# A channel-attention kernel: other piece sizes in its first pass, and other first stores and reads

## The chip, the cores and the metric

The kernel runs on one core of a Trainium2 chip. The metric is device time in microseconds, from one execution's start to its end. The kernel before takes 733.99 us as the median of three runs (733.06, 733.99, 737.35).

## The reference

The input x has 384 x 384 pixels of 384 channels in bf16. Each channel gets one factor from its mean and its maximum over all pixels, and x is multiplied by these factors. No pixel can be scaled before all have been seen.

```python
def reference(x, w1, w2):            # x (1, 384, 384, 384), w1 (384, 96), w2 (96, 384)
    B, H, W, C = x.shape
    xf = x.reshape(B, H * W, C)
    gap = jnp.mean(xf, 1)
    gmp = jnp.amax(xf, 1)
    h_a = gap @ w1
    h_a = h_a * (h_a > 0)
    h_m = gmp @ w1
    h_m = h_m * (h_m > 0)
    scale = _sigmoid(h_a @ w2 + h_m @ w2)
    return x * scale[:, None, None, :]
```

## The kernel before

**Tiling.** The pixels lie on 128 partitions, and each partition has 1,152 of them. One pixel on all partitions is called a row here: 128 x 384 values, 98,304 bytes. x is 1,152 rows, 113.25 MB. On-chip memory does not hold that, so there are two passes.

**First pass** (lines 366 to 399). One list, `loads`, is made from the constants at the top and then walked in order. SyncE issues each load (line 369). TensorE adds its rows up with matmuls against a column of ones (line 274, groups of four rows, three matmuls each). VectorE takes the maximum of its rows with an accumulator `acc` in the tensor `hole`, 11 rows wide, in instructions of 6 and 5 rows by turns (line 311, `larger`). Toward the end the accumulator is folded to 6 and then 3 rows (`FOLDS`: key, how many loads are left; value, the new width), and then to one.

**Slots.** Three slots of 44 rows hold what is loaded; the trace calls them x_88, x_89 and x_90, and they are used in turn. `FILLS` has one entry per use of a slot: a first tuple of packed pieces (16 rows, a pair of two packed groups of 8) and a second of plain pieces. The plain pieces of the fills, 804 rows, are read again in the second pass (`AGAIN`), and so are the 11 rows that the accumulator starts from; everything else stays on the chip. A piece may be loaded once all engines that read what was in its rows are done, and the order of SyncE's queue is that of the list: a load that waits holds up the ones behind it. Besides, at most eight DMAs are under way: a load also waits for the landing of the eighth before it.

**Packing** (`pack`, line 316). 144 rows stay on the chip in a shorter code. For a pair of groups ScalarE takes the bytes apart (line 321), TensorE joins the high parts (line 334, three groups of six matmuls into one bank, each taken out by ScalarE at line 344), ScalarE copies the low bytes (line 339; with the second of these copies the slot's 16 rows are read for the last time) and tests the result (lines 341 and 346). The working space for that lies in the first rows of `room`, which take plain rows later (`ROOM_PIECES`), after the last pair.

**What stays.** 44 rows in each slot (`STAYING`), 35 in `room`, 10 beside the accumulator (`LATE_PIECES`, put into the list at the place that `LATE_AT` names: slot, and how many of its pieces go before), 16 in PSUM. The list ends with the third slot's pieces. The last three loads are summed in another form (`tail_sums`).

**Between the passes.** After the last maximum: a fold to one row, transposes, two small products and a sigmoid (lines 404 to 425) give `scale_bc`.

**Second pass** (lines 481 to 532). VectorE multiplies a piece in place (line 430), ScalarE's queue issues its store (line 446), and SyncE reads the next block into the slot once the store has landed (line 454). `FIRST_STORES` cuts the first slots and the room into stores, `FIRST_READS` the first reload, taken from the slot's end. Later ones are of 44 rows. The packed rows are unpacked between them.

Scheduling of the first pass is left to the framework, within each engine by the order of the program; for the second pass it is written out by hand.

Of the kernel before, what the change touches and what calls it, by code (L numbers as in the profile page):

```python
# [54 lines left out]

PSUM_PIECES = (4, 12)
FILLS = (
    ((16,), ()), ((), (44,)), ((), (44,)), ((16,), ()), ((), (44,)), ((), (44,)),
    ((16,), ()), ((), (44,)), ((), (44,)), ((16,), ()), ((), (44,)), ((), (44,)),
    ((16,), ()), ((), (44,)), ((), (44,)), ((16,), ()), ((), (43,)), ((), (40,)),  # L60
    ((), (36,)), ((), (36,)), ((16,), (27,)), ((), (28,)), ((), (28,)), ((16,), (26,)),
    ((), (24,)), ((), (23, 21)), ((16,), (16,)), ((), (16,)),
)
ROOM_PIECES = (10, 9, 5, 6, 5)
STAYING = ((17, 15, 12), (11, 11, 11, 11), (6, 4, 3, 4, 3, 6, 3, 3, 3, 6, 3))
ROOM_LOADS = 2
LATE_AT = (2, 1)
LATE_PIECES = (5, 5)

FOLDS = {7: 6, 1: 3}  # L70

AGAIN = (44,) * 18 + (12,)
FIRST_STORES = ((1, 2, 3, 4, 4, 6, 8, 8, 8), (8, 8, 9, 9, 10), (10, 11, 14))
FIRST_READS = ((8, 8, 8, 10, 10), (44,))
LEAD = 2
ROOM_TURN = 2
ACC_STORES_AT = 3
# [8 lines left out]
def kernel(  # L86
# [158 lines left out]
    def pieces_of(block, pieces, buf):  # L245
        j = 0
        for m in pieces:
            loads.append((block, j, j + m, buf, j, ()))
            j += m
        assert j == block[1]  # L250

    for s, pieces in enumerate(STAYING):
        if s == ROOM_LOADS:
            pieces_of(room_b, ROOM_PIECES, room)
        n = len(loads)
        pieces_of(stay_b[s], pieces, slots[s])
        if s == LATE_AT[0]:
            j = 0
            for i, m in enumerate(LATE_PIECES):
                loads.insert(n + LATE_AT[1] + i, (late_b, j, j + m, late, j, ()))  # L260
                j += m
# [95 lines left out]
    def fold(n, to):  # L357
        while n > to:
            h = min(n // 2, n - to)
            larger(acc[:, 0:h, :], acc[:, 0:h, :], acc[:, n - h:n, :])  # L360
            n -= h
        return n
# [3 lines left out]
    for i, (block, lo, hi, buf, at, groups) in enumerate(loads):  # L366
# [14 lines left out]
        if i == len(PSUM_PIECES):  # L381
# [5 lines left out]
            continue  # L387
        if n_loads - i in FOLDS:
            width = fold(width, FOLDS[n_loads - i])
            parts, turn = PARTS[width], 0  # L390
# [91 lines left out]
    order.insert(ROOM_TURN, (room_b, None))  # L482
    stores, reads = list(FIRST_STORES), list(FIRST_READS)
    n_turns = len(order) + len(again)
# [92 lines left out]
```

## Time and profile before

The profiled execution took 734.48 us, with a span of 732.6 us and 1.9 us around it.

| what | number |
| --- | --- |
| median of three runs | 733.99 us (733.06 to 737.35) |
| profiled execution, its span | 734.48 us, 732.6 us |
| bytes moved | 193.51 MB read, 113.25 MB written; 419 GB/s over the span |
| VectorE busy | 556.5 us (76%) |
| ScalarE busy | 250.8 us (34%) |
| TensorE busy | 162.8 us (22%) |
| chain of waits, by kind | DMA 58%, VectorE 34%, issue 2% |
| the last load of the first pass lands | 274.03 us |
| `scale_bc` is ready | 280.34 us |
| first store is issued | 280.75 us |

How to read it: times within the execution count from the span's start. "Busy" is time in which an engine works on an instruction. The chain of waits is followed from the last instruction back to what released it, step by step, and so names what the end of the execution hung on. A load's landing is the last of sixteen completion signals, one from each DMA engine.

### The profile page before, as it was taken

What the parts mean: (1) busy time and instruction counts of PE and PEld (TensorE: products, weight loads), DVE (VectorE), ACT (ScalarE), POOL (GpSimd) and SP (SyncE); (2) the same over time, 40 slices, a digit from 0 to 9 for tenths busy, and PEclk for the clock granted to TensorE, in tenths of its full rate; (3) what the DMA queues carried; (4) which work ended last, traced back from release to release, by engine and by line L of the source; (5) the groups of instructions that cost most, each with busy time, mean ns of one, the idle gap of its engine ahead of it and who ended that gap; (6) DMA issues with size and microseconds to landing.
All of it is one profiled execution on the core that took longest, in us unless ns stands there. A gap on an engine that the chain in (4) does not pass through costs nothing.

```text
span 732.6 us, 3124 instructions
## 1 busy us (share of the span) xinstructions
PE 162.8 (22%) x1069; PEld 52.0 (7%) x1078; DVE 556.5 (76%) x422; ACT 250.8 (34%) x135; POOL 0.7 (0%) x6
## 2 busy tenths in 40 slices
PE   3664656554756561000000000000000000000000
PEld 0221212111211120000000000000000000000000
DVE  6689989899999998979276777277667666667930
ACT  4998889853997400002011011011110011111100
POOL 0000000000000000000000000000000000000000
PEclk9968878677675755555555555555555555555555
DMA  9999999999999988999999999999999999999997
GB/s 378 440 431 414 431 415 412 400 426 427 427 424 422 417 329 306 386 442 425 437 439 424 435 436 441 421 437 440 424 437 437 423 437 439 423 437 427 434 438 339
DMA packets 19391, 306.95 MB, mean 419 GB/s; under 512 B 2512, under 2 KB 3120, under 8 KB 8368
## 3 DMA queue, kind: packets, MB, share of 16 engines
q1 hardware_dynamic: 12896, 193.52, 62.5%
q10 hardware_dynamic: 6480, 113.25, 36.2%
q8 instruction: 8, 0.13, 0.1%
q14 instruction: 7, 0.06, 0.0%
HBM read 193.51 MB, written 113.25 MB: 419 GB/s over the span
## 4 chain that ended last, share of the span: by engine, by line
DMA 58%; DVE 34%; issue 2%; ACT 0%; SPq 0%; PE 0%; DVEq 0%; ACTq 0%
DMA x<-in_x_dram 37%; DMA out_dram<-x 21%; DVE hole L311 20%; DVE x L430 12%; DVE room L430 1%; DVE hole L430 1%; ACT room L464 0%; SPq L369 0%; DVE room L470 0%; DVEq L535 0%; PE bank_a L424 0%; ACT scale_bc L425 0%; DVE small L419 0%; PE bank_a L418 0%; PE bank_a L422 0%
## 5 line engine op out<-in xcount | busy, mean ns | idle before, releaser
L430 DVE TENSOR_TENSOR x<-x,scale_bc 128x16896 bf16<-128x16896 bf16 (+9 forms) x34 | 191.5, 5660 | 94.6 <-DMA x<-in_x_dram 93.5
L311 DVE TENSOR_TENSOR hole<-hole,x 128x1920 bf16<-128x1920 bf16 (+2 forms) x211 | 235.7, 1191 | 20.0 <-DMA x<-in_x_dram 18.6
L464 ACT ACTIVATE room<-room 128x3072 uint16<-128x3072 uint8 x18 | 49.7, 2763 | 360.2 <-DVE x L430 309.4
L274 PE MATMUL bank_a<-x,small 128*1 128x512 bf16 (+1 forms) x816 | 92.7, 481 | 49.4 <-DMA x<-in_x_dram 48.6
L334 PE MATMUL bank_b<-room 128*128 128x512 bf16 x153 | 59.9, 526 | 51.9 <-ACT room L324 22.4
L321 ACT CAST room<-x 128x3072 bf16<-128x3072 uint8 x18 | 48.7, 2750 | 45.1 <-DMA x<-in_x_dram 45.1
L339 ACT COPY room<-x 128x3072 uint8<-128x3072 uint8 x18 | 49.3, 2737 | 0.0
L470 DVE TENSOR_TENSOR room<-room,hole 128x3072 uint16<-128x3072 uint16 x18 | 31.6, 1758 | 23.0 <-ACT room L464 23.0
L341 ACT ACTIVATE room<-room,w_sb 128x6144 uint8<-128x6144 bf16 x9 | 48.7, 5407 | 0.0
L430 DVE TENSOR_TENSOR room<-room,scale_bc 128x3072 bf16<-128x3072 bf16 (+3 forms) x21 | 38.9, 1861 | 0.6
L274 PEld LDWEIGHTS <-small 128*1 128x1 bf16 x861 | 29.1, 95 | 131.8 <-issue 116.0
L467 DVE TENSOR_SCALAR hole<-room 128x768 uint16<-128x768 uint16 x90 | 25.7, 353 | 0.0
L346 ACT ACTIVATE room<-room,w_sb 128x3072 bf16<-128x3072 uint16 x9 | 25.7, 2853 | 0.0
L334 PEld LDWEIGHTS <-room 128*128 128x128 bf16 x162 | 19.0, 119 | 90.9 <-issue 85.7
L344 ACT ACTIVATE room<-bank_b 128x512 uint16<-128x512 f32 x27 | 15.9, 590 | 1.7 <-PE bank_b L334 1.7
L324 ACT ACTIVATE room<-x 128x1536 bf16<-128x1536 bf16 x9 | 13.3, 1478 | 0.0
L470 DVE TENSOR_TENSOR hole<-hole 128x768 uint16<-128x768 uint16 x18 | 10.0, 558 | 0.6
L299 ACT COPY w_sb<-bank_a 65x128 f32<-65x128 f32 x2 | 0.5, 262 | 25.3 <-PE bank_a L274 24.8
L311 DVE TENSOR_TENSOR hole<-hole,room 128x1920 bf16<-128x1920 bf16 (+2 forms) x7 | 7.6, 1152 | 0.0
L379 DVE COPY kept_ps<-x 128x768 uint32<-128x768 uint32 (+1 forms) x2 | 3.5, 1760 | 4.2 <-DMA x<-in_x_dram 4.2
L274 PE MATMUL bank_a<-room,small 128*1 128x512 bf16 (+1 forms) x27 | 4.1, 543 | 4.2 <-DMA room<-in_x_dram 4.2
L311 DVE TENSOR_TENSOR hole<-hole 128x1920 bf16<-128x1920 bf16 (+2 forms) x6 | 4.9, 823 | 0.1
(46 smaller groups left out, 29.8 us busy)
## 6 DMA issues: line engine op xcount, KB each, us to landing
x<-in_x_dram SPq DMA_DIRECT2D x27, 4224.0 KB, 24.4
out_dram<-x ACTq DMA_DIRECT2D x19, 4224.0 KB, 24.0
x<-in_x_dram SPq DMA_DIRECT2D x11, 1536.0 KB, 12.2
x<-in_x_dram SPq DMA_DIRECT2D x2, 3456.0 KB, 16.7
out_dram<-room ACTq DMA_DIRECT2D x2, 3072.0 KB, 31.4
x<-in_x_dram SPq DMA_DIRECT2D x2, 2688.0 KB, 16.7
x<-in_x_dram SPq DMA_DIRECT2D x4, 1056.0 KB, 11.4
out_dram<-room ACTq DMA_DIRECT2D x1, 4224.0 KB, 29.5
```

The source lines that it names most:

```text
L274: nc.tensor.matmul(sum_ps[q * QP:q * QP + 1, 0:g * P], lhsT=ones_bf[:, 0:1], rhs=rows[:, :, q * P:(q + 1) * P], start=(summed == 0), stop= ...
L311: nc.vector.tensor_tensor(out=out, in0=a, in1=b, op=ALU.max)
L321: nc.scalar.copy(out=lanes[:, h], in_=halves[:, h, :, :, 1].rearrange("p (w g) c -> p w (g c)", g=n_grp))
L334: nc.tensor.matmul(pack_ps, lhsT=diag[:, w, :], rhs=flat(src)[:, i * 512:(i + 1) * 512], start=(w == 0), stop=(w == len(WEIGHTS) - 1),)
L339: nc.scalar.copy(out=planes(k + i)[0], in_=halves[:, i, :, :, 0])
L341: nc.scalar.activation(out=flat(test).bitcast(U8), in_=flat(high), func=ACT.Abs, bias=middle, scale=1.0 / STEP)
L344: nc.scalar.activation(out=code[:, i * 512:(i + 1) * 512], in_=pack_ps, func=ACT.Copy, bias=-OFFSET)
L346: nc.scalar.activation(out=flat(test), in_=flat(test).bitcast(U16), func=ACT.Square, bias=good, accum_out=flags[:, k // 2:k // 2 + 1],)
L430: nc.vector.tensor_tensor(out=dst, in0=src, in1=scale_bc.unsqueeze(1).to_broadcast([P, n, C]), op=ALU.mult)
L464: nc.scalar.activation(out=words, in_=low, func=ACT.Copy, bias=float(HIGH))
L467: nc.vector.tensor_scalar(out=out, in0=code, scalar1=shift, scalar2=mask, op0=op, op1=ALU.bitwise_and)
L470: nc.vector.tensor_tensor(out=out, in0=a, in1=b, op=ALU.bitwise_or)
```

## The change

The constants of the first pass get other values, with the same total of rows. A packed pair shares its slot with plain rows: most fills that held 16 packed rows alone now hold 16 and 20 to 28 plain rows (the last one two plain pieces of 12 and 16). The number of fills goes from 28 to 25, and that of first-pass loads from 60 to 64. All pairs are in slot x_90, where the last three were in x_89. The pieces that stay are cut otherwise; the 10 late rows come in one load, among the pieces of the second slot instead of the third. The fold to 6 rows comes two loads earlier. In the second pass the first stores and the first reload have fewer and larger pieces.

```diff
 PSUM_PIECES = (4, 12)
 FILLS = (
-    ((16,), ()), ((), (44,)), ((), (44,)), ((16,), ()), ((), (44,)), ((), (44,)),
-    ((16,), ()), ((), (44,)), ((), (44,)), ((16,), ()), ((), (44,)), ((), (44,)),
-    ((16,), ()), ((), (44,)), ((), (44,)), ((16,), ()), ((), (43,)), ((), (40,)),
-    ((), (36,)), ((), (36,)), ((16,), (27,)), ((), (28,)), ((), (28,)), ((16,), (26,)),
-    ((), (24,)), ((), (23, 21)), ((16,), (16,)), ((), (16,)),
+    ((16,), ()), ((), (40,)), ((), (44,)), ((16,), (28,)), ((), (44,)), ((), (44,)),
+    ((16,), (28,)), ((), (43,)), ((), (27,)), ((16,), (27,)), ((), (44,)), ((), (44,)),
+    ((16,), (28,)), ((), (36,)), ((), (40,)), ((16,), (20,)), ((), (36,)), ((), (32,)),
+    ((16,), (28,)), ((), (27,)), ((), (28,)), ((16,), (24,)), ((), (23, 21)), ((), (20,)),
+    ((16,), (12, 16)),
 )
-ROOM_PIECES = (10, 9, 5, 6, 5)
-STAYING = ((17, 15, 12), (11, 11, 11, 11), (6, 4, 3, 4, 3, 6, 3, 3, 3, 6, 3))
+ROOM_PIECES = (8, 6, 5, 6, 5, 5)
+STAYING = ((16, 14, 14), (11, 11, 11, 6, 5), (4, 4, 3, 3, 6, 6, 3, 3, 6, 3, 3))
 ROOM_LOADS = 2
-LATE_AT = (2, 1)
-LATE_PIECES = (5, 5)
-
-FOLDS = {7: 6, 1: 3}
+LATE_AT = (1, 3)
+LATE_PIECES = (10,)
+
+FOLDS = {9: 6, 1: 3}
 
 AGAIN = (44,) * 18 + (12,)
-FIRST_STORES = ((1, 2, 3, 4, 4, 6, 8, 8, 8), (8, 8, 9, 9, 10), (10, 11, 14))
-FIRST_READS = ((8, 8, 8, 10, 10), (44,))
+FIRST_STORES = ((4, 4, 4, 7, 8, 8, 9), (10, 11, 11, 12), (16, 19))
+FIRST_READS = ((10, 11, 11, 12), (44,))
```

## The prediction

> **What bounds the kernel now.** I began with the page's slices. The three rows are the busy share of VectorE, that of the 16 DMA engines, and what these moved, in forty slices of 18.3 us:
>
> ```profile
> DVE  6689989899999998979276777277667666667930
> DMA  9999999999999988999999999999999999999997
> GB/s 378 440 431 414 431 415 412 400 426 427 427 424 422 417 329 306 386 442 425 437 439 424 435 436 441 421 437 440 424 437 437 423 437 439 423 437 427 434 438 339
> ```
>
> The DMA engines are never idle for long, so time is bytes over rate, and what can be won lies where the rate falls: slices 2 to 14 (first pass, 400 to 431), 15 to 17 (between the passes), the last. I then asked for stretches: the first five rounds of loads, the quiet rest of the first pass, its end, the first stores, the second pass. Columns: us, busy time of each engine, clock, DMA share, GB/s.
>
> ```profile
> 23.20:48.20 25.00, 15.34 (x98) 5.08 (x100) 22.29 (x19) 23.05 (x12) 0.00 (x0) 0.81 1.01 430
> 121.00:147.00 26.00, 16.87 (x99) 5.37 (x100) 22.28 (x19) 23.27 (x12) 0.00 (x0) 0.70 0.99 402
> 172.50:195.20 22.70, 14.68 (x98) 4.63 (x99) 22.64 (x21) 18.33 (x8) 0.00 (x0) 0.79 1.00 428
> 252.70:271.00 18.30, 10.52 (x72) 2.09 (x66) 18.21 (x19) 0.00 (x0) 0.00 (x0) 0.62 1.02 402
> 271.00:280.40 9.40, 5.31 (x60) 3.95 (x56) 7.28 (x15) 1.78 (x7) 0.00 (x0) 0.50 0.46 147
> 280.40:305.00 24.60, 0.00 (x0) 0.00 (x0) 24.60 (x18) 0.00 (x0) 0.00 (x0) 0.50 0.94 357
> 305.00:700.00 395.00, 0.00 (x0) 0.00 (x0) 277.31 (x168) 49.74 (x18) 0.00 (x0) 0.50 1.01 433
> ```
>
> From 305 us on 433 GB/s flow without a break, whatever is queued; the change touches nothing there. VectorE is busy 22.3 us of a round (third figure after the comma), near the DMA's own need but under it. The chain of waits of the first pass (start, us, what) shows what a round waits for:
>
> ```profile
> 23.23 9.45 DVE hole L311 x8
> ...
> 32.75 15.48 DMA x<-in_x_dram
> ...
> 57.84 14.26 DMA x<-in_x_dram
> ...
> 130.61 16.40 DMA x<-in_x_dram
> ```
>
> A slot lands, VectorE takes its maxima in 9.45 us, only then is its next load issued, and that lands 14.3 to 16.4 us later. The waits of SyncE, which issues all loads in order, say the same, with the second cause, the packed pairs:
>
> ```profile
> SPq L369 <- DVE hole L311: 174.2, 33, 10.8
> SPq L369 <- ACT room L339: 44.7, 9, 9.1
> ```
>
> Last, the DMA queues: q8 is instruction code, eight packets of 16 KB.
>
> ```profile
> q1 hardware_dynamic: 12896, 193.52, 62.5%
> q8 instruction: 8, 0.13, 0.1%
> ```
>
> **The loss in a round.** Loads queued close behind one another land 10.03 us apart for 44 rows (23.14 to 33.17) and 3.69 for 16 (33.17 to 36.86). An undisturbed round of 44+44+16 rows takes 10.03+10.03+3.69 = 23.75. The five rounds from 23.14 to 147.01 took 123.87; four of 23.75 and one with 43 rows (23.52) are 118.5. So 5.4 us were lost. Afterwards little is: from the landing at 156.10 to the last, at 274.03, the slowest of the 16 engines took 117.9 and the earliest 117.7 (the trace has one completion signal per engine).
>
> What differs is how early a load is issued. I call lead the time from its issue to the landing of the load ahead of it. Before: x88 lands at T, is reissued at T+9.6, and ahead of it are x89 and the pair, 10.03+3.69 = 13.7; lead 4.1 (trace: 36.86-32.75 = 4.11; the ten 44-row loads have 4.1 to 5.7). From 155 us on leads are 5.6 to 14, and the order of the 16 signals keeps still; with leads of 4 it is reshuffled each round, and the first and last signal of a load drift apart, from 0.53 us (landing 23.14) to 3.94 (147.01). So engines run dry waiting for a load that waits for the slowest. That is one part of the loss: the earliest engine lost 2.0 of the 5.4. The rest is that the slowest engine falls back further: at 48.23 fifteen signals lie within 0.54 us and the last 1.35 behind, just after the code packet at 37.45.
>
> **The change part by part.**
>
> Slots. x90 takes a pair and a 28-row piece, so a full round is 44+44+16+28 rows. x88 is still reissued at T+9.6, but ahead of it are 10.03+3.69+6.40 = 20.1 (28 rows: 6.40, landings 182.41 to 188.82); lead 10.5. The pair's 16 rows are released 12.6 us after landing (36.86 to 49.46, L339), with 28+44+44 rows ahead, 26.5; lead 13.9. The shortest is the pair behind 28+27+28 rows: 19.0-12.6 = 6.4. No lead is under 6, where the trace of before shows no loss (188.91, lead 6.3: spread 3.00 before, 2.92 after). SyncE passes the new 28-row issue in 0.4 us; behind it wait x88 and x89, which have 10 us to spare.
>
> What of the 5.4 comes back? All of it if short leads caused everything. Code packets remain, since PE's instruction count is the same. The first cost the last landing 1.35; the four that fell into the well-led stretch (168, 199, 228, 263 us) each set one engine back by some 1.5, but only that at 228 hit one far behind and moved the last landing, by 0.66. I leave 1.35+0.66 = 2.0 in place; the ends are 0 and 1.35 plus two more on the same engine, 4.1. Gain 3.4 (1.3 to 5.4).
>
> The Trainium skill's page Runtime: NRT & Kernel Launch, Instruction fetch mechanics, says that each sequencer refills in 16 KiB blocks over a DMA queue of its own and that this is mostly hidden. The sequencer's side no row here shows; for the DMA engine that carries the block the trace disagrees (1.35 us above). By that rule 2.0 would be 0, the case of the first rival below.
>
> Sizes. Four more loads (64 for 60), fewer of 44 rows. Per row 28 rows cost 0.2286 us, 44 rows 0.2280, 16 rows 0.2306, 11 rows 0.2336. Over all pieces that comes to +0.3 (0 to 0.6).
>
> The Trainium skill's page DMA: Bandwidth & Descriptors, Anatomy of one DMA, gives each DMA about 2.0 us fixed besides bytes over 436 GB/s (fitted on another issue path), 8 us for four more loads. The spacing in the trace disagrees: 44 rows (4.33 MB) would take 11.9 and take 10.03.
>
> Packing. ScalarE needs 21.9 us for a pair (13.14 to 35.1); the shortest round between pairs is 99 rows, 22.6, so it keeps up. On PE, 19 sums of the new 28 rows now stand ahead of the second group of packing matmuls. They need the landing, 6.4 us after the pair's; the group waits for ScalarE till about 10 anyway (36.86 to 46.86). Cost 0; without that cover each us would lengthen the pair by one. After the last pair 126 rows, 29 us, pass before the room loads, which need 18.7 us of packing: 0.
>
> VectorE. Fewer instructions (eight), same rows. With 104 rows in 23.75 us and 22.3 busy it still waits for loads. At the very end, pieces 6, 3, 3 follow instead of 3, 6, 3: one 3-row maximum (pitch 0.67) fewer between the last landing but one and the last fold. Now 274.03 to 277.60 passes there; gain 0.3 (0 to 0.7). The earlier fold is 1.2 us with two more loads to catch up in: 0.
>
> First stores and reads. The first product has 4 rows (0.95) instead of 1 (0.36), so the first store goes 0.6 us later; but packets of 768 to 2,304 bytes vanish from a stretch that ran at 338 to 400 GB/s. The last store of x88 has 9 rows for 8, so its first reload goes 0.2 to 0.4 later; one reload DMA and one room store fewer. In 24.6 us this stretch loses 24.6 x (1-357/433) = 4.3 in all. I take 0, with 1 either way.
>
> Sum: 3.4-0.3+0.3+0 = 3.4 gained. The profiled execution took 734.48 (span 732.6, 1.9 around it), 0.5 above the median of 733.99. So 731.1 for such an execution, 730.6 as a median; bounds 733.99-7.1 = 726.9 and 733.99+0.3 = 734.3.
>
> **Rivals.** (1) Code packets cost nothing once leads are long: 5.4-0.3+0.3 = 5.4 gained, 728.6, with sizes and stores up to 726.9. For it: the signals keep still after 155 us. Against: the lone late signal at 48.23. Chance 0.15.
>
> (2) The change lengthens leads but the time does not follow: the whole 5.4 belongs to one slow engine. 733.5 to 734.5. For it: at 48.23 only one engine was late. Against: 2.0 lost by the earliest, and the quiet second half. Chance 0.14.
>
> (3) Slower: each load pays its start. The lone first load took 3.40 us for 4 rows (0.91), 2.5 of start. Were this paid for four more loads, it is 10.0 less 3.4: 740.6, and more if pairs in the short rounds are released later than I reckon. It decides once a lead falls below 2.5. Against: 6.4 is the shortest, and queued loads land spaced by their size alone (10.03 and 3.69 above). Chance 0.07.
>
> **How the numbers follow.** My case (729 to 733) has 0.62, the rivals 0.15, 0.14 and 0.07, 0.02 is unexplained. The time is 730.6. The range is that of the sum's bounds, 727.0 to 734.4: it holds my case, (1) and nearly all of (2), some 0.88, and leaves out (3). One per cent, 7.3 us, is what a measurement here can tell: faster means below 726.7, past the end of rival (1), 0.06; slower above 741.3, half of (3) and the unexplained, 0.05; within, 0.89.
>
> **What would show it.** Right: rounds of the first pass at 430 GB/s, no slot landing 14 us or more behind its issue as a link of the chain there, a spread of signals near 2 at the end, last load near 270.6 instead of 274.03, scale near 276.7 instead of 280.34, 433 GB/s after. Wrong: landings still more than 10.1 us apart for 44 rows; a SyncE wait for the packing longer than 10 us; a gap in DMA at the first reloads longer than now.

## The result, and the profile after

The changed kernel takes 729.81 us as the median of 20 runs (729.36 to 734.88), the kernel before 733.81 us in 20 runs beside it (732.24 to 737.35). The ratio is 0.9955, with a 95% interval of 0.9944 to 0.9967: 4.0 us or half a per cent less, inside the one per cent that was taken for no change. The profiled execution of the changed kernel took 729.56 us, with a span of 727.8 us, 4.8 us less than before.

| us | before | after | earlier or less by |
| --- | --- | --- | --- |
| last load of the first pass lands | 274.03 | 270.14 | 3.89 |
| from there to the last fold's end | 3.57 | 3.35 | 0.22 |
| `scale_bc` is ready | 280.33 | 276.21 | 4.12 |
| from there to the end of the span | 452.30 | 451.57 | 0.73 |

So of the 4.85 us by which the two profiled spans differ (the medians differ by 4.0), 3.9 came out of the first pass's loads, 0.2 out of its last pieces, and 0.7 out of the second pass. The stretches of the changed kernel show the same (columns as in the prediction: us, busy time of TensorE, its weight loads, VectorE, ScalarE, GpSimd with the number of instructions, clock, DMA share, GB/s):

```profile
22.20:128.40 106.20, 62.88 (x425) 20.07 (x430) 97.87 (x86) 82.77 (x43) 0.00 (x0) 0.79 1.00 428
128.40:270.10 141.70, 82.55 (x561) 26.31 (x565) 139.95 (x133) 105.13 (x61) 0.00 (x0) 0.75 1.00 418
276.20:305.00 28.80, 0.00 (x0) 0.00 (x0) 28.76 (x16) 0.01 (x1) 0.00 (x0) 0.50 0.96 380
305.00:700.00 395.00, 0.00 (x0) 0.00 (x0) 274.53 (x166) 49.73 (x18) 0.00 (x0) 0.50 1.00 433
```

The first pass now runs at 428 GB/s up to 128 us (before 423), and from 121 to 147 us, where the kernel before was down to 402, at 429; its smaller pieces behind that run at 418, much as before (419). In the last stretch the 433 GB/s of before stand again. In the first 24.6 us of the stores 371 GB/s flow (before 357).

The chain of waits of the changed kernel (start, us, what) has a link of another kind in the first pass:

```profile
25.67 10.23 DMA x<-in_x_dram
...
35.92 5.41 ACT room L321 x2
...
45.85 2.65 ACT room L339
...
48.52 18.91 DMA x<-in_x_dram
...
80.04 13.46 DMA x<-in_x_dram
```

It no longer goes through VectorE's maxima (9.45 us a round before) but through ScalarE's packing, whose copy at line 339 releases the pair's 16 rows. Their next load then lands 10.2 to 18.9 us later. That is no stall: it is issued that early, and the loads ahead of it in the queue fill the time.

The waits of SyncE, which issues the loads (what it waited for: us in all, times, the longest):

```profile
SPq L369 <- DVE hole L311: 164.7, 35, 11.7
SPq L369 <- ACT room L339: 37.5, 8, 7.8
```

The longest wait for the packing went from 9.1 to 7.8 us, although a 28-row load now stands between. Once the slots are filled, the shortest lead (issue of a load to the landing of the load ahead) is 6.39 us, at 187.44 us; in the rounds up to 128 us leads are 6.5 to 16.2, where those of the large loads were 4.1 to 5.7.

What this did can be seen in the sixteen completion signals of single loads, which are sorted here by time within the load. Five loads of before, then five of the changed kernel: the time of the first signal, and how far the third, the ninth and the last four lie behind it, in us.

```
before   first   3rd  9th  13th 14th 15th 16th
        36.33   0.19 0.28 0.33 0.50 0.52 0.53
        46.34   0.19 0.29 0.50 0.54 0.54 1.89
        94.12   0.09 0.41 1.50 1.53 1.76 2.04
       118.40   0.06 0.85 1.38 1.54 1.62 2.62
       143.07   0.03 0.44 0.81 1.79 2.39 3.94
after
        35.47   0.11 0.18 0.27 0.31 0.35 0.43
        41.89   0.10 0.17 0.30 0.34 0.43 1.79
        97.93   0.09 0.23 1.23 1.51 1.80 1.84
       128.16   0.03 0.20 1.10 1.45 1.66 1.68
       195.72   0.03 0.76 1.69 1.71 1.76 1.80
```

Up to the last loads shown, code packets of 16 KB fell at 37.45, 66.25, 104.18 and 136.31 us before, at 36.06, 67.60, 97.63, 134.12, 164.46 and 193.08 after. In both kernels the first puts one engine 1.4 us behind the rest. After that the pictures part. In the changed kernel each further packet takes another engine out of the close group and sets it beside the one already late, so the sixteenth signal stays at 1.7 to 1.8 us (2.06 at the end of the pass, by another kind of packet that E6 below shows). Before, the offsets are reshuffled from load to load, and the sixteenth drifts to 3.94.

### The profile page after: what moved, and what is told of

It reads as the page before. It is cut to its first block, busy times and chain, and to the rows that moved or that the text cites. A ratio compares the mean times of both kernels' runs of the same rounds, so it can differ in the third digit from the quotient of the medians.

```text
span 727.8 us, 3125 instructions
## 1 busy us (share of the span) xinstructions
PE 156.4 (21%) x1069; PEld 50.5 (7%) x1078; DVE 556.4 (76%) x422; ACT 250.3 (34%) x135; POOL 0.7 (0%) x6
## 4 chain that ended last, share of the span: by engine, by line
DMA 60%; DVE 18%; ACT 14%; issue 2%; PE 1%; SPq 0%; DVEq 0%; ACTq 0%
DMA x<-in_x_dram 39%; DMA out_dram<-x 21%; DVE x L430 12%; ACT room L321 6%; ACT room L339 5%; DVE hole L311 5%; ACT room L324 2%; DVE room L430 1%; PE bank_b L334 1%; DVE hole L430 1%; ACT room L344 1%; PE bank_a L274 1%; ACT room L464 0%; DVE room L470 0%; SPq L369 0%
## 5 line engine op out<-in xcount | busy, mean ns | idle before, releaser
L430 DVE TENSOR_TENSOR x<-x,scale_bc 128x16896 bf16<-128x16896 bf16 (+7 forms) x31 | 191.3, 6194 | 93.5 <-DMA x<-in_x_dram 92.4
L311 DVE TENSOR_TENSOR hole<-hole,x 128x1920 bf16<-128x1920 bf16 (+3 forms) x215 | 235.8, 1175 | 15.8 <-DMA x<-in_x_dram 14.3
L274 PE MATMUL bank_a<-x,small 128*1 128x512 bf16 x816 | 95.2, 492 | 59.5 <-DMA x<-in_x_dram 59.0
L334 PE MATMUL bank_b<-room 128*128 128x512 bf16 x153 | 52.0, 465 | 43.8 <-ACT room L324 20.7
L430 DVE TENSOR_TENSOR room<-room,scale_bc 128x3072 bf16<-128x3072 bf16 (+2 forms) x20 | 38.9, 1947 | 0.6
L334 PEld LDWEIGHTS <-room 128*128 128x128 bf16 x162 | 17.1, 109 | 78.0 <-issue 70.4
L311 DVE TENSOR_TENSOR hole<-hole,room 128x2304 bf16<-128x2304 bf16 (+2 forms) x7 | 7.7, 1156 | 0.0
L311 DVE TENSOR_TENSOR hole<-hole 128x384 bf16<-128x384 bf16 (+4 forms) x6 | 4.9, 823 | 0.1
```

The lines of the kernel that those rows point to most:

```text
L274: nc.tensor.matmul(sum_ps[q * QP:q * QP + 1, 0:g * P], lhsT=ones_bf[:, 0:1], rhs=rows[:, :, q * P:(q + 1) * P], start=(summed == 0), stop= ...
L311: nc.vector.tensor_tensor(out=out, in0=a, in1=b, op=ALU.max)
L334: nc.tensor.matmul(pack_ps, lhsT=diag[:, w, :], rhs=flat(src)[:, i * 512:(i + 1) * 512], start=(w == 0), stop=(w == len(WEIGHTS) - 1),)
L430: nc.vector.tensor_tensor(out=dst, in0=src, in1=scale_bc.unsqueeze(1).to_broadcast([P, n, C]), op=ALU.mult)
```

## The experiments

**Theory.** A code packet sets one DMA engine back, and with short leads that setback reaches the other fifteen, since the next load waits for the slowest; with long leads it stays with its engine. **Rivals:** short leads cost time by themselves; every further load costs its start; the cut into pieces, not the leads, brings the gain; the first stores bring part of it. Ratios are against the kernel before, run beside each.

**E1 and E2: the two halves of the change.** E1 is the changed kernel with the old stores and reads, E2 the kernel before with the new ones:

```diff
-FIRST_STORES = ((1, 2, 3, 4, 4, 6, 8, 8, 8), (8, 8, 9, 9, 10), (10, 11, 14))
-FIRST_READS = ((8, 8, 8, 10, 10), (44,))
+FIRST_STORES = ((4, 4, 4, 7, 8, 8, 9), (10, 11, 11, 12), (16, 19))
+FIRST_READS = ((10, 11, 11, 12), (44,))
```

> The changed kernel with the first stores and reads of before (FIRST_STORES, FIRST_READS). Theory: longer leads in the first pass give the whole gain, the stores 0: 729.8 us, 4.0 below before. Rival: the larger first stores give the 0.7 us by which the changed profile's second pass is shorter: 730.5 us, 3.3 below.

> The kernel before with only the first stores and reads changed. Theory: no change, 733.8 us (within 0.3). Rival (the stores give 0.7 us): 733.1 us. If the later first store cost something: 734.4 us.

E1: 732.01 us in 12 runs, 0.9985 (0.9973 to 0.9997). Its last load lands at 269.99 and `scale_bc` is ready at 276.04, as in the changed kernel, but of the four microseconds won there only 1.1 (by the ratio) to 1.8 (by the medians) are left at the end; both values that were expected, 729.8 and 730.5, are missed. E2: 735.36 us in 12 runs, 1.0020 (1.0000 to 1.0039), slower than was expected. So the two halves do not add up: the stores cost the old first pass 1.6 us and save the new one about 2.

**E3: the fills alone.** Only `FILLS` is changed; the pieces that stay, the late rows, the folds and the stores are those of before.

> The kernel before with only FILLS changed; the staying, room and late pieces, the folds and the first stores are those of before. Theory (leads): nearly all of the gain, 730.1 us, the end of the pass giving back 0.3; last landing at 270.1 to 270.6, the spread of its signals near 2. Rival (the pieces at the end of the pass, the later fold and the one late load bring it): 733 us or more, last landing above 273.

730.6 us in 12 runs, 0.9972 (0.9955 to 0.9989). The last load lands at 270.14, to the hundredth where it does in the changed kernel, with a spread of 2.30 us. All that the loads gained comes from `FILLS`. `scale_bc` is ready at 276.42, 0.21 after that of the changed kernel, which is the worth of the other end of the pass.

**E4: long leads without other slots.** The kernel before, with the 44-row pieces of the first fifteen fills in two halves (ten more loads, where the expectation says 12), so that the first half is issued while the second is still being reduced:

```diff
-    ((16,), ()), ((), (44,)), ((), (44,)), ((16,), ()), ((), (44,)), ((), (44,)),
+    ((16,), ()), ((), (22, 22)), ((), (22, 22)), ((16,), ()), ((), (22, 22)), ((), (22, 22)),
...
```

> The kernel before with each 44-row load of the first pass cut into two of 22 rows; pairs stay alone in their slots. Half a slot is free while VectorE still reads the other half, so by the prediction's rules the leads in the first five rounds become 7.6 to 14 us with no change of slots. Theory (leads alone): the gain comes back but for the smaller packets, 0.5 to 0.9 us: 730.3 to 730.8 us. Rival (a start paid by each of the 12 more loads, 2.5 us each): above 740 us. Rival (it takes the sharing of slots): 733.8 us.

732.4 us in 12 runs, 0.9990 (0.9975 to 1.0006), above the 730.3 to 730.8 that were expected; the last load lands at 270.57 and the spread is 2.10 us. The chain of waits of E4:

```profile
51.08 11.30 DMA x<-in_x_dram
...
74.99 11.30 DMA x<-in_x_dram
...
98.90 11.30 DMA x<-in_x_dram
```

The reader is to see the starts: 23.91 us apart, round after round, against the 23.75 of an undisturbed round in whole pieces, while code packets fell at 66.52 and 99.96. The signals show these packets: at 65.56 one lies 1.86 behind, at 70.61 two (1.68 and 1.88), at 104.63 three (1.68, 1.72, 1.88). With leads of 7.6 to 14 us, won in quite another way, the same happens as in the changed kernel, and although E4 has ten loads more than before, its last landing is 3.5 us earlier: a load's start is not paid again. `scale_bc` is ready at 276.88, 3.5 us earlier too, but by the medians only 1.4 us of that are left at the end, and by the ratio no gain is shown; in the profiled execution the second pass gives 1.4 us back (452.15 us from `scale_bc` to the last store's landing, 450.72 before).

**E5 and E6: short and long leads with few code packets.** Most of TensorE's sums are left out, so that 241 matmuls remain of 1,069, and two 16 KB code packets of eight. E5 does it to the kernel before, E6 to the changed one:

```diff
+    def summed_at(i):
+        return i < 3 or i == n_loads - SUM_TAIL - 1
...
-        for r in to_sum[i]:
-            sums(buf[:, r[0]:r[1], :], TOT - tail_rows)
+        if summed_at(i):
+            for r in to_sum[i]:
+                sums(buf[:, r[0]:r[1], :], few)
```

> The kernel before, leaving out most of the sums of the first pass (only those of the first three loads, of the last regular one and of the three tail loads are made), so TensorE has about a quarter of its instructions and 2 or 3 instead of 8 code packets of 16 KB go over the DMA engines; loads, maxima and packing are the same and leads stay near 4 us. Theory (a code packet sets one engine back by 1.4 us, and short leads make all others wait for it): with the packets gone most of the 5.4 us comes back, last landing 269 to 270.5, time 729.3 to 730.5 us. Rival (short leads alone make the engines run dry): loss stays, last landing above 273, time 733 to 734 us.

> The changed kernel with the same sums left out. Theory: the 1.4 to 2.0 us that the code packets still cost there goes: last landing 268.4 to 268.9 with a spread of its signals of 0.5 to 1, time 728.0 to 728.6 us. Rival (code packets cost nothing with long leads, the late signals have another cause): spread still near 2, time 729.5 to 730 us.

E5: 731.22 us in 11 runs, 0.9953 (0.9930 to 0.9976), above the time that was expected, though its last load lands where it was expected, at 270.26. Its code queue in the view of DMA queues (packets, MB, share):

```profile
q8 instruction: 2, 0.03, 0.0%
```

And its chain of waits (line 316 is line 311 of before):

```profile
23.24 9.45 DVE hole L316 x8
...
32.70 14.19 DMA x<-in_x_dram
...
56.45 15.07 DMA x<-in_x_dram
...
81.09 14.19 DMA x<-in_x_dram
```

The leads are as short as before: a slot lands, is reduced for 9.45 us, and its load lands 14.19 us after its issue. From the landing at 23.14 to the one at 46.89 are 23.75 us, exactly the undisturbed round, and the spread stays at 0.45 us until 60 us. A lead of 4.2 us costs nothing by itself, and this rival falls. The second round takes longer, and the trace has the reason: a smaller code packet, 8 KB, at 68.83 us, after which one signal lies 1.34 behind. The third round has leads of 4.2 us and one engine 1.34 behind, and takes 23.76 us; the fourth has the 16 KB packet at 98.76 us and takes 24.22. The five rounds take 120.12 us instead of 123.87; 118.5 would be undisturbed. That TensorE reads less in E5 is not the reason: in the first round of the kernel before, with 98 matmuls, the first signals come 23.73 us apart (22.61 to 46.34), in E5 23.74.

What short leads do once an engine is late shows in E5 between 98.76 and 200.17 us, where no code packet falls. Five of its loads, columns as above; the leads of the second to fourth are 4.2 us, those of the loads from there to the fifth 6.5 and more:

```
E5     first    3rd  9th  13th 14th 15th 16th
       117.75   0.07 0.16 0.36 0.60 1.26 1.75
       127.81   0.06 0.20 1.07 1.23 1.35 1.72
       141.55   0.06 0.68 1.56 1.59 1.59 1.70
       150.74   0.22 1.02 1.51 1.52 1.53 1.65
       189.87   0.22 1.03 1.51 1.52 1.53 1.66
```

Engines that were close to the first fall back toward the late one, without a packet of their own, and stop doing so when leads are long. The landing itself loses nothing by that (119.50 to 143.26 are 23.76 us). What is lost is the distance between these engines and the last one, and the next packet can then set back an engine that is late already; that this is how the kernel before lost its 5.4 us is a reading that no run shows step by step.

E6: 730.52 us in 12 runs, 0.9956 (0.9940 to 0.9972), not the 728.0 to 728.6 that were expected. The expectation that its last load would land at 268.4 to 268.9 failed too: 270.34, with a spread of 2.30. One 16 KB packet is left in its first pass, at 106.56 us, and that one alone puts an engine 1.8 us behind; the eight of the changed kernel do no more, since they go to different engines, as far as sorted signals can tell. The rest up to 2.30 comes from 8 KB packets (queue q14 of the trace, four in the first pass). The last three signals of a load behind the first one, around two such packets:

```
E6     packet 67.20:   0.57 0.61 0.70  ->  0.63 0.71 1.38
E6     packet 197.94:  0.67 1.35 1.83  ->  0.67 1.83 2.32
```

An engine near 0.41 goes to 1.38 at the first, and 1.35 becomes 2.32 at the second: 0.97 both times. The same step is in the changed kernel (1.10 vanishes and 2.08 appears after the packet at 197.74), in E8 below (1.04 and 2.01) and in E3 (1.30 and 2.27). It fits one engine that is hit twice, and it is this engine that ends the first pass in all four.

**E8, E9, E10: the changed kernel, E1 and E2 again**, on another chip, since E1 and E2 rested on differences of 2 us; **E7** is the kernel before with the new `FILLS`, stores and reads, but the old pieces that stay.

> The changed kernel once more, beside the next three on one chip. Expected as before: 729.8 us (729.5 to 730.3), scale ready at 276.0 to 276.6.

> The changed kernel with the first stores and reads of before, a second time. Theory (the new stores save 0.65 us of DMA time after the scale, and the spread of the second pass's end does the rest by chance): 730.5 us, 0.7 above the changed kernel. Rival (with the old stores the second pass is really 2 us longer): 732 us again.

> The kernel before with only the new first stores and reads, a second time. Theory as above: 733.2 us, 0.6 below before. Rival (the new stores cost time on the old first pass): 735 us again, with stretches under 420 GB/s between 315 and 365 us in the profile.

> The kernel before with the new FILLS and the new first stores and reads; the pieces that stay, the room's, the late ones and the folds are those of before. Theory: all of the gain but the 0.2 us of the end of the pass: 730.0 us. Rival (the stores are worth nothing without the new end of the pass): 730.6 us or more, as with the new FILLS alone.

| kernel | first pass | stores | median, us | ratio, 95% |
| --- | --- | --- | --- | --- |
| E8 | new | new | 730.0 (7 runs) | 0.9944 (0.9924 to 0.9965) |
| E9 | new | old | 731.74 (12) | 0.9964 (0.9948 to 0.9979) |
| E10 | old | new | 735.9 (12) | 1.0027 (1.0004 to 1.0051) |
| E7 | new fills | new | 730.23 (6) | 0.9941 (0.9918 to 0.9964) |

The order repeats: new stores save about 1.7 us behind the new first pass and cost 1.9 behind the old one, though for the saving the intervals of E8 and E9 overlap (those of the changed kernel and E1 do not). E7 cannot be told from the changed kernel. E3 does not fit the order well: it too has the new fills and the old stores, and its median is 730.6, though its interval overlaps those of E1 and E9.

Where the difference lies is seen in the second pass. The stretch from 345 to 365 us (columns as above), first of the kernel before:

```profile
345.00:365.00 20.00, 0.00 (x0) 0.00 (x0) 6.69 (x9) 2.76 (x1) 0.00 (x0) 0.50 1.00 433
```

The same stretch of E2:

```profile
345.00:365.00 20.00, 0.00 (x0) 0.00 (x0) 6.59 (x9) 2.76 (x1) 0.00 (x0) 0.50 1.00 406
```

And of E10:

```profile
345.00:365.00 20.00, 0.00 (x0) 0.00 (x0) 6.14 (x9) 2.76 (x1) 0.00 (x0) 0.50 0.99 406
```

The share of busy DMA engines is one in all three (0.99 in E10), yet 406 instead of 433 GB/s flow: 20 x (1-406/433) = 1.25 us. The engines are not idle there: single packets take longer. A packet of 33,792 bytes (one partition's 44 rows) takes 1.25 us in the second pass of every kernel, but between 300 and 400 us 48 of them take 1.4 to 2.4 us in E2 and 50 in E10, in bursts near 321, 350 and 360 us; before has one such packet, the changed kernel three, E1 and E8 none. In E2 these take 23.9 us more than 1.25 each, 1.5 us for each of the 16 engines. E4 and E5, with the old stores, have 29 and 22, so it is not the new stores alone that bring them on.

The other two terms are what the DMA engines lose against 433 GB/s from `scale_bc` to 310 us, and the spread of the last store's signals at the end:

| us | first stores' loss | spread at the end | `scale_bc` to last store's landing |
| --- | --- | --- | --- |
| before | 4.50 | 1.74 | 450.72 |
| E2 | 3.75 | 2.62 | 452.17 |
| E10 | 3.51 | 3.55 | 453.28 |
| after | 3.80 | 1.13 | 449.42 |
| E8 | 3.72 | 1.28 | 449.56 |
| E1 | 4.58 | 2.90 | 451.97 |
| E9 | 4.61 | 1.31 | 450.26 |

From before to E2 the terms give -0.75 + 0.88 + 1.25 = 1.4 of the 1.45 us; from after to E1 0.78 + 1.77 = 2.55, all of it. From before to E10 they give 2.1 of 2.56. So the new stores save 0.7 to 1.0 us at once, in every pair; the rest is the slow packets, where there are any, and how far the engines are apart at the end, which differs from kernel to kernel and, between E1 and E9, from one profiled execution to the next.

**E11 and E12: an earlier first reload of the second slot.** In the changed kernel and in E6, E7 and E8 the load of that slot was issued 6.8 to 7.1 us before the landing of the load ahead, in the others 4.4 to 5.5, so the same rule as in the first pass might hold. E11 is the changed kernel, E12 is E2, both with this reload cut and taken from the slot's start, whose rows are stored first:

```diff
-FIRST_READS = ((10, 11, 11, 12), (44,))
+FIRST_READS = ((10, 11, 11, 12), (10, 11, 11, 12))
...
+        if up:
+            j = 0
+            for m in pieces:
+                nc.sync.dma_start(out=buf[:, j:j + m, :], in_=part(xr, block, j, j + m))
+                j += m
+            assert j == block[1]
+            return
...
-        get(block, slots[s], reads.pop(0) if reads else (block[1],))
+        get(block, slots[s], reads.pop(0) if reads else (block[1],), up=(s == 1))
```

> The changed kernel with the first reload of the second slot cut into four pieces, in the order of its stores, so that each piece goes out as soon as its own rows are stored and not after the slot's last store. Leads of the first reloads grow from 6.9 us to over 10. Theory (short leads there set the engines out of step, and the changed kernel has just enough): little to win, 729.3 to 729.8 us, no stretch under 425 GB/s after 300 us. Rival (leads play no part in the second pass): 729.9 us with the same rates. Against it: two more loads among the eight that may be under way could hold up stores, 731 us.

> The first pass of before with the new first stores and reads, and the same early reload. Theory (its loss of 1.5 to 2 us came from the reload issued 5 us ahead): the dips between 315 and 365 us go, 733.2 us, 0.6 below before. Rival (the new stores cost time on the old first pass for another reason): 735.5 us and the dips again.

E11: 731.84 us in 12 runs (729.48 to 739.84), 0.9981 (0.9948 to 1.0014), not better than the changed kernel. E12: 734.4 us in 12 runs, 0.9987 (0.9965 to 1.0009); from 350 to 375 us it still moves only 419 GB/s (before 433, E2 411), with 27 slow packets. An earlier reload does not cure the second pass, and its lead is not what decides: E1, E3 and E9, with 4.4 to 5.5 us, have three slow packets at most. Why some packets take longer there stays open. Nothing that was run can be told to be faster than the changed kernel.

## Why the prediction was right, and where it was not

**The leads.** Right in kind. They grew to 6.39 us and more, and the drift of the signals ended. The term was 3.4 us; the last landing came 3.89 earlier, and if the 0.3 reckoned against it for sizes is right, which no run isolates, it measured 4.2. E5 shows what the prediction had left open, that short leads and code packets are needed together: leads of 4.2 us lose nothing until a packet sets one engine back, and then other engines fall back toward it. The five rounds of the kernel before lost 1.34, 0.11, 0.33, 1.10 and 2.47 us, while the packets fell in the first, second, fourth and fifth; so these are not four equal setbacks, and 0.78 of the last round was lost by two loads (landings 131.69 and 135.52) while no code packet fell. Nor is the rule for the lead known between 4.2 and 6.4 us: the load that the kernel before issued at 236.83 us had a lead of 5.60 behind a spread of 3.46, and no offset moved, but it has only 11 rows.

**What is left in place.** The prediction left 2.0 us for code packets, as 1.35 + 0.66. Measured from the spreads it is 2.06 - 0.43 = 1.6 us. The size was near, but the reason held only in part: setbacks of different engines do not add up behind long leads, and the engine that is last at the end is one that two 8 KB packets hit, which the prediction did not look at.

The Trainium skill's page Runtime: NRT & Kernel Launch, section Instruction fetch mechanics, gives blocks of 256 instructions and calls the cost of crossing one mostly hidden. TensorE's 2,147 matmuls and weight loads make 8.4 such blocks, and the trace has eight packets; E5's 482 make 1.9, and it has two. Whether it is hidden from the engine that fetches no row here shows. From the DMA engine that carries the block it is not (the spread grows by 1.36 us from 35.47 to 41.89 in the changed kernel), and with short leads not from the kernel: E5, with six of them fewer, has its last landing at 270.26 instead of 274.03.

**Sizes, packing, VectorE.** As reckoned: queued loads land spaced by their size (E4 too), SyncE's wait for the packing got shorter, and the maxima dropped out of the chain in the rounds. Not as reckoned is the count of VectorE's instructions: instead of eight fewer there are 422 as before, 215 for 211 of them maxima of loaded rows in the slots, and the busy time is the same (556.4 us for 556.5). **The end of the pass:** 0.3 us was predicted, 0.22 measured (E3 against the changed kernel: 0.21).

**First stores and reads: this step failed.** It was "I take 0, with 1 either way", beside "433 GB/s flow without a break, whatever is queued; the change touches nothing there". The stores' own stretch gained 0.7 us. But the second pass does depend on what went before it: E2 and E10 fell to 406 GB/s in it, with packets of up to 2.4 us, and the stores were worth from 1.9 us lost to about 2 gained. With the new first pass and the old stores E1 and E9 took 732 us, inside the range but 1.1 to 1.4 above the forecast (E3 took 730.6). That the forecast came within 0.8 us of 729.81 is therefore in part luck: the prediction had no reason for what the stores are worth behind this first pass, and none is known now.

**The rivals.** (1), code packets cost nothing behind long leads: near, since most of the 5.4 us came back, but 1.6 us stayed, and 728.6 was not reached. (2), the time does not follow the leads: refuted by E3 and E4. (3), each load pays its start: refuted, with ten more loads E4 was through 3.5 us earlier.

**The signs named ahead.** 430 GB/s in the rounds (428), a spread near 2 (2.06), the last load near 270.6 (270.14), the scale near 276.7 (276.21) and 433 GB/s afterwards all came. "No slot landing 14 us or more behind its issue as a link of the chain" was the wrong sign: long leads make that time longer, and the chain has links of 17.3 and 18.9 us in loads that lose nothing. The lead itself, or the spread of the signals, is the sign to ask for.

## What to carry to other kernels

A DMA-bound loop needs more than enough queued bytes on average: each load must be issued so early that the engines that are ahead stay busy while a late one is still at the load before, here, for the large loads, more than 4.2 us before the landing ahead of it, and 6.4 us was enough. Compare the sixteen completion signals of a load from round to round: offsets that stand still mean that a disturbance stays with its engine, offsets that are reshuffled mean that others pay for it. And follow a gain to the end of the kernel before counting it: here some 4 us in the middle were between 1 and 4 at the end, with one cause of the difference, the slow packets, still unexplained.

## What was not expected of the hardware

- A 16 KB code packet takes 0.9 to 1.2 us on its DMA engine and sets it back by some 1.55 us, for the rest of the pass (from 0.23 to 1.79 behind the first signal at 36.06 us in the changed kernel, from 0.21 to 1.75 at 98.76 in E5); an 8 KB one takes 0.3 to 0.45 us and sets it back by 0.97 or, near 215 us, by 0.7 (0.08 to 0.79 in the changed kernel). Both are more than the packet's own time.
- In the changed kernel the 16 KB packets went to another engine each time; the 8 KB packets near 67 and 197 us hit the same one in four kernels, as far as sorted signals can tell.
- Offsets between engines stand still to 0.01 us over 88 us of queued loads (0.76, 1.10, 1.44 and 1.67 among the signals of the load whose first lands at 108.03 us in the changed kernel, 0.76, 1.10, 1.45 and 1.67 at 195.72), so nothing brought a late engine back into step while the queue was that deep.
- The DMA share of a stretch can be one while the rate is 6% down (406 of 433 GB/s), because single packets take up to 2.40 us instead of 1.25.
